# Decode attention and MLP on one core: weights loaded partition-major, K and P transposed on VectorE, scores by a block-diagonal q

## The chip, the cores and the metric

The kernel runs on one core of a Trainium2 chip. The metric is device time in microseconds (us). "Median" below is over the executions of one kernel. An execution counts as slow when it is over 1.5% above the fastest of the same kernel; comparisons use fast executions alone. A profile shows one execution, and its span is about 1.8 us shorter than the measured time (102.4 us against 104.2 us for the kernel before).

Names: PE is TensorE, PEld its weight loads, DVE VectorE, ACT ScalarE, POOL GpSimd, SP SyncE. A "q" after a name (ACTq) means that engine's own instruction stream, where it issues DMAs. L409 is line 409 of that kernel's own source, so the same work has other line numbers in other kernels.

## The reference

One token passes through attention over the last 4096 keys and through an MLP, both fed by the same normalised x, and both are added to x.

```python
# x (1,1,1024); wq (1024,4096); wo (4096,1024); w1 (1024,3584); w2 (3584,1024)
# caches (1,4,65536,128), only the last W=4096 rows are read; 32 q heads, 4 kv heads
xn = layernorm(x)
q  = (xn @ wq), as 32 heads of 128
o  = softmax(q . k^T * 128**-0.5) . v          # each kv head serves 8 q heads
y  = layernorm(xn)
out = x + o @ wo + (gelu(y @ w1 + b1) @ w2 + b2)
```

All data is bfloat16. The kernel must read 39.86 MB (the profile's own count): wq 8.4, w1 7.3, K 4.2, V 4.2, w2 7.3 and wo 8.4 MB. Each weight is used for one row only, so this is a streaming job with a chain of dependent steps hanging on it.

## The kernel before

The parts that matter. Weights are loaded row-block by row-block, so for wq, w1 and wo a run of contiguous memory for one partition is one row (8, 7 and 2 KB).

```python
WO_CHUNKS = [4, 4, 4, 4, 4, 4, 4, 3, 1]
W2_CHUNKS = [9, 9, 8, 2]
# SP issues the loads in this order: Wq, W1, K, V, W2, WO
for k in range(KC):
    sp.dma_start(WA[:, k * NQ:(k + 1) * NQ], A_wq[k * 128:(k + 1) * 128, :])
for k in range(KC):
    sp.dma_start(W1[:, k * F:(k + 1) * F], B_w1[k * 128:(k + 1) * 128, :])
# ... K and V: 32 keys of one partition are 8 KB in one run ...
# ... W2: nch rows of one partition in one run; WO:
sp.dma_start(WA[:, h0 * D:(h0 + nh) * D].rearrange("p (h n) -> p h n", h=nh),
             A_wo[h0 * 128:(h0 + nh) * 128, :].rearrange("(h d) n -> d h n", h=nh))
```

Rows become columns, and K becomes K transposed, on TensorE; the copies out of PSUM are shared by VectorE and ScalarE:

```python
for h in range(32):                                   # q row -> QT, 128x32
    pe.matmul(PSb[...], lhsT=Qrow[0:1, h*128:(h+1)*128], rhs=identb[0:1, 0:1], is_transpose=True)
for bb in range(16):                                  # 8 units of 16 K blocks
    pe.matmul(PSb[:, col0:col0+128], lhsT=KT[:, ...128 columns...], rhs=identb, is_transpose=True)
# ... copies PSUM -> KT on DVE and ACT ...
for g in range(HKV):                                  # scores: 128 small matmuls
    for b in range(NBLK):
        pe.matmul(PS[:, ...8 columns...], lhsT=KT[:, block b], rhs=QT[:, g*8:(g+1)*8])
# ... max, subtract, exp ...
w2_chunk_mms(pe, 0)          # 18 W2 matmuls sit here, under the softmax and before PV
for g in range(HKV):                                  # PV: 128 small matmuls
    for b in range(NBLK):
        pe.matmul(PS[:, ...8 columns...], lhsT=V[:, block], rhs=Pb[:, ...8 columns...])
# OT (128 x 32, one column per head) = PV result * 1/sum   -> already in the layout WO needs
for j in range(1, len(W2_CHUNKS)):
    w2_chunk_mms(pe, j)
# ... 64 WO matmuls with lhsT=OT[:, h:h+1], then copy and one output DMA
```

## Time and profile before

| | before |
|---|---|
| median time | 104.28 us (104.22 to 104.4) |
| span of the profile | 102.4 us |
| HBM read | 39.86 MB, 389 GB/s over the span |
| bulk packets in the trace: first start, last end | 1.75 us, 98.5 us |
| TensorE busy | 81.3 us, 79% |
| exp ends | 65.8 us |
| last matmul ends | 100.1 us |

The page of the kernel before, its 40 slices of 2.56 us each: busy tenths of TensorE, the granted TensorE clock in tenths, the mean busy share of the 16 DMA engines, and the rate.

```profile
PE   0021899999559998849999856489999999999991
...
PEclk9999999999999999995999955559995999999999
DMA  2999999999999999999999999999999999999910
GB/s 38 406 414 426 426 438 416 426 426 431 420 434 421 423 417 433 432 435 413 422 422 419 416 457 396 461 461 408 416 373 408 403 408 410 407 410 410 366 54 1
```

The DMA row is the one to read: 9 in every slice but the first and the last two. The stream never pauses. TensorE has free time, but next to none after the softmax, from 67 us on.

The page of the kernel before, the chain of waits that ended last, by engine and by line:

```profile
DMA 49%; PE 34%; SPq 14%; issue 1%; DVE 1%
DMA W<-in_B_w_dram 49%; PE PS L409 15%; PE PS L633 14%; SPq L160 10%; SPq L157 4%; PE PS L578 3%; PE PS L310 2%; DVE ROW L650 1%; PE PS L588 0%; PE PS L562 0%
```

Half of it is DMA, then the W2 matmuls (L409) and the WO matmuls (L633): the job is over when the last weights have come and been used.

The timeline of the kernel before; columns are start (us), length (us), engine, line, operation, output and inputs, shape and count, then idle time before it and what ended it.

```profile
56.90 3.41 PE L480 MATMUL PS<-QT,KV 128*128 128x8 bf16 x128 [0.42 <-DVE KV L454]
...
64.82 1.02 ACT L533 ACTIVATE Pb<-PS 128x1024 bf16<-128x1024 f32 x1 [7.26 <-DVE PS L524]
...
66.96 5.34 PE L409 MATMUL PS<-W,GT 128*1 128x512 bf16 x18 [1.88 <-DMA W<-in_B_w_dram]
...
72.30 3.37 PE L578 MATMUL PS<-Pb,KV 128*128 128x8 bf16 x128
...
75.93 10.05 PE L409 MATMUL PS<-W,GT 128*1 128x512 bf16 x38
...
85.81 14.31 PE L633 MATMUL PS<-WA,OT 128*1 128x512 bf16 x64
...
100.16 0.68 DVE L650 CAST ROW<-PS 1x512 bf16<-1x512 f32 x1 [23.64 <-PE PS L633]
```

Scores (L480) end at 60.3, exp (L533) at 65.8, 18 of the W2 matmuls run before PV (L578), PV takes 3.4 us, and from 66.96 to 100.1 TensorE is practically never idle. So the kernel before is balanced: the stream ends at 98.5 us, and TensorE has just caught up with it. Note that the 18 W2 matmuls took 5.34 us, which is 297 ns each, where 64 WO matmuls took 14.31 us, 224 ns each: their first part ran at the slower clock (the PEclk row has 5 up to the slice that ends at 69.1 us; the matmuls start 427 ns apart there, and 216 later).

### The profile page before, as it was taken

Reading aid. Unit: us, or ns where it says so; the run is one execution under the profiler, and the core shown is the slowest. Engines: PE = TensorE matmul, PEld = TensorE weight load, DVE = VectorE, ACT = ScalarE, POOL = GpSimd, SP = SyncE. Lnnn points to the kernel's source line nnn. Section 1 sums busy time; section 2 is a strip of 40 time slices with the busy share of each in tenths; the row PEclk is TensorE's granted clock in tenths of the full one; section 3 lists DMA queues with packets and bytes.
Section 4 is the critical chain, followed back from the end, with each engine's and each line's share of the span. In section 5 each row is a group of like instructions: output and inputs, shape, how many; then the busy total and the mean of one; then the engine's idle time right before and its main releaser. Section 6 shows DMA issues by size and latency. Waiting matters only on the chain.

```text
span 102.4 us, 1568 instructions
## 1 busy us (share of the span) xinstructions
PE 81.3 (79%) x700; PEld 41.1 (40%) x700; DVE 22.0 (21%) x47; ACT 14.1 (14%) x16; POOL 3.5 (3%) x14
## 2 busy tenths in 40 slices
PE   0021899999559998849999856489999999999991
PEld 0020333333123331339999753023872333333320
DVE  0016400000440000074759444540110000000002
ACT  5000510000420000053337400300000000000002
POOL 5700000000000000000000000000000000000000
PEclk9999999999999999995999955559995999999999
DMA  2999999999999999999999999999999999999910
GB/s 38 406 414 426 426 438 416 426 426 431 420 434 421 423 417 433 432 435 413 422 422 419 416 457 396 461 461 408 416 373 408 403 408 410 407 410 410 366 54 1
DMA packets 8407, 39.95 MB, mean 390 GB/s; under 512 B 721, under 2 KB 721, under 8 KB 5970
## 3 DMA queue, kind: packets, MB, share of 16 engines
q1 hardware_dynamic: 8274, 39.85, 94.5%
q8 instruction: 5, 0.08, 0.3%
q0 software_dynamic: 128, 0.01, 0.1%
HBM read 39.86 MB, written 0.00 MB: 389 GB/s over the span
## 4 chain that ended last, share of the span: by engine, by line
DMA 49%; PE 34%; SPq 14%; issue 1%; DVE 1%
DMA W<-in_B_w_dram 49%; PE PS L409 15%; PE PS L633 14%; SPq L160 10%; SPq L157 4%; PE PS L578 3%; PE PS L310 2%; DVE ROW L650 1%; PE PS L588 0%; PE PS L562 0%
## 5 line engine op out<-in xcount | busy, mean ns | idle before, releaser
L409 PE MATMUL PS<-W,GT 128*1 128x512 bf16 x56 | 15.4, 443 | 1.9 <-DMA W<-in_B_w_dram 1.9
L283 PE MATMUL PS<-WA,XNTb 128*1 128x512 bf16 x64 | 16.0, 417 | 0.3 <-DVE msy L244 0.3
L310 PE MATMUL PS<-W,YTb 128*1 128x512 bf16 x56 | 12.7, 379 | 3.5 <-DVE ROW L293 2.4
L633 PE MATMUL PS<-WA,OT 128*1 128x512 bf16 x64 | 14.3, 379 | 0.0
L439 PE MATMUL PS<-identb,KV 128*128 128x128 bf16 x128 | 9.1, 243 | 1.5 <-ACT ROW L336 1.5
L409 PEld LDWEIGHTS PS<-W,GT 128*1 128x1 bf16 x56 | 5.2, 95 | 12.1 <-issue 7.3
L283 PEld LDWEIGHTS PS<-WA,XNTb 128*1 128x1 bf16 x64 | 5.7, 90 | 10.2 <-issue 2.9
L439 PEld LDWEIGHTS PS<-identb,KV 128*128 128x128 bf16 x128 | 8.8, 111 | 1.6 <-ACT ROW L336 1.6
L310 PEld LDWEIGHTS PS<-W,YTb 128*1 128x1 bf16 x56 | 4.4, 83 | 11.9 <-DVE ROW L293 2.9
L633 PEld LDWEIGHTS PS<-WA,OT 128*1 128x1 bf16 x64 | 5.2, 84 | 8.9 <-DMA WA<-in_A_wo_dram 1.0
L454 DVE COPY KV<-PS 128x1024 bf16<-128x1024 bf16 x10 | 6.3, 685 | 2.3 <-PE PS L439 2.3
L466 ACT ACTIVATE KV<-PS 128x1024 bf16<-128x1024 bf16 x6 | 5.9, 1019 | 3.3 <-PE PS L439 3.3
L650 DVE CAST ROW<-PS 1x512 bf16<-1x512 f32 x1 | 0.7, 678 | 23.6 <-PE PS L633 23.6
L293 DVE CAST ROW<-PS 1x2048 bf16<-1x2048 f32 x1 | 2.3, 2278 | 14.8 <-PE PS L283 14.8
L177 PE MATMUL PS<-identb,X 8*128 8x8 bf16 x1 | 0.2, 181 | 6.5 <-DMA X<-in_A_x_dram 6.5
L644 ACT ACTIVATE ROW<-PS 1x512 bf16<-1x512 f32 x1 | 0.6, 586 | 34.3 <-PE PS L633 34.3
L298 ACT ACTIVATE ROW<-PS 1x2048 bf16<-1x2048 f32 x1 | 1.9, 1866 | 13.8 <-PE PS L283 13.8
L480 PE MATMUL PS<-QT,KV 128*128 128x8 bf16 x128 | 3.4, 167 | 0.4 <-DVE KV L454 0.4
L480 PEld LDWEIGHTS PS<-QT,KV 128*128 128x128 bf16 x128 | 3.3, 98 | 0.6 <-DVE KV L454 0.6
L336 ACT ACTIVATE ROW<-PS 1x1536 bf16<-1x1536 f32 x1 | 1.4, 1439 | 15.3 <-PE PS L323 15.3
L331 DVE COPY QT<-PS 128x32 bf16<-128x32 bf16 x1 | 0.2, 192 | 14.8 <-PE PS L323 14.8
L578 PE MATMUL PS<-Pb,KV 128*128 128x8 bf16 x128 | 3.4, 166 | 0.0
(77 smaller groups left out, 37.8 us busy)
## 6 DMA issues: line engine op xcount, KB each, us to landing
WA<-in_A_wq_dram SPq DMA_DIRECT2D x8, 1024.0 KB, 11.7
W<-in_B_w_dram SPq DMA_DIRECT2D x8, 896.0 KB, 25.4
WA<-in_A_wo_dram SPq DMA_DIRECT2D x7, 1024.0 KB, 15.1
W<-in_B_w_dram SPq DMA_DIRECT2D x2, 2304.0 KB, 26.2
KV<-in_A_k_cache_dram SPq DMA_DIRECT2D x4, 1024.0 KB, 26.2
KV<-in_A_v_cache_dram SPq DMA_DIRECT2D x4, 1024.0 KB, 27.1
W<-in_B_w_dram SPq DMA_DIRECT2D x1, 2048.0 KB, 33.1
WA<-in_A_wo_dram SPq DMA_DIRECT2D x1, 768.0 KB, 12.7
```

The source lines that it names most:

```text
L157: sp.dma_start(WA[:, k * NQ:(k + 1) * NQ], A_wq[k * 128:(k + 1) * 128, :]).then_inc(s_wq[k], 16)
L160: sp.dma_start(W1[:, k * F:(k + 1) * F], B_w1[k * 128:(k + 1) * 128, :]).then_inc(s_w1[k], 16)
L283: last = pe.matmul(PS[0:1, n * 512:(n + 1) * 512], lhsT=XNTb[:, k:k + 1], rhs=WA[:, k * NQ + n * 512: k * NQ + (n + 1) * 512], start=(k == ...
L293: STATE["d_qrow0"] = DVE.mark(dve.tensor_copy(Qrow[:, 0:2048], PS[0:1, 0:2048]))
L310: last = pe.matmul(PS[0:1, (n + 1) * 512:(n + 2) * 512], lhsT=YTb[:, k:k + 1], rhs=W1[:, k * F + n * 512: k * F + (n + 1) * 512], start=(k ...
L409: pe.matmul(PS[0:1, 6 * 512 + n * 512: 6 * 512 + (n + 1) * 512], lhsT=GT[:, c:c + 1], rhs=reg[:, n * 512:(n + 1) * 512], start=False, stop ...
L439: last = pe.matmul(PSb[:, col0: col0 + 128], lhsT=KT[:, g * W + b * 128: g * W + (b + 1) * 128], rhs=identb[:, :], is_transpose=True)
L454: last = dve.tensor_copy(KT[:, g * W + (hu * 16 + 8 * s_) * 128: g * W + (hu * 16 + 8 * s_ + 8) * 128], PSb[:, bk * 1024:(bk + 1) * 1024])
L466: STATE["a_ktcopy"][u] = ACT.mark(act.activation(out=KT[:, g * W + (hu * 16 + 8) * 128: g * W + (hu * 16 + 16) * 128], in_=PSb[:, bk * 102 ...
L480: last = pe.matmul(PS[:, bank_base + b * 8: bank_base + (b + 1) * 8], lhsT=KT[:, g * W + b * 128: g * W + (b + 1) * 128], rhs=QT[:, g * 8: ...
L578: last = pe.matmul(PS[:, 4 * 512 + g * REP: 4 * 512 + (g + 1) * REP], lhsT=V[:, (g * NBLK + b) * DH:(g * NBLK + b + 1) * DH], rhs=Pb[:, (g ...
L633: last = pe.matmul(PS[0:1, 6 * 512 + n * 512: 6 * 512 + (n + 1) * 512], lhsT=OT[:, h:h + 1], rhs=WA[:, h * D + n * 512: h * D + (n + 1) * ...
```

## The change

The intent is to make the DMA stream cheaper and to take the transposes off TensorE:

1. Each partition gets a block of consecutive rows of a weight (partition p holds rows 8p to 8p+7 of wq), so one run of wq is 16 KB where it was 8, of w1 14 where it was 7, and of wo 16 (10, 4 and 2 in the last chunks) where it was 2. W2, K and V were in long runs already. W1 now comes before Wq.
2. That order of rows wants x, h and the attention output in "p-major" order. Small DMAs from the ScalarE queue, on the chip or from HBM, spread rows over partitions: x, b1, h (HTb), q (Q2), and four for the attention output (OT).
3. K and P are transposed on VectorE in 32x32 blocks. The blocks are not put in their final place; instead a block-diagonal q (QBD) makes a 128-row matmul that gives the scores of all heads at once, and PV uses 32 matmuls of 512 columns with a mask that picks each head's own kv group.
4. The first W2 chunk no longer runs before PV: all W2 matmuls come after it.

The diff, cut to its core (`# ...` marks cuts; the setup, norms and GELU change little):

```diff
-WO_CHUNKS = [4, 4, 4, 4, 4, 4, 4, 3, 1]
-W2_CHUNKS = [9, 9, 8, 2]
+W1_CHUNKS = [2, 2, 2, 2]
+WQ_CHUNKS = [2, 2, 2, 2]
+W2_CHUNKS = [8, 8, 8, 4]
+WO_CHUNKS = [8, 8, 8, 5, 2, 1]
 # ... loads: W1 first, long runs
-            for k in range(KC):
-                sp.dma_start(WA[:, k * NQ:(k + 1) * NQ],
-                             A_wq[k * 128:(k + 1) * 128, :]).then_inc(s_wq[k], 16)
+    wq_p = A_wq.rearrange("(p k) n -> p (k n)", k=KC)
+    wo_p = A_wo.rearrange("(p j) n -> p (j n)", j=OC)
+            for i, c0, n in cuts(W1_CHUNKS):
+                sp.dma_start(W1[:, c0 * F:(c0 + n) * F], w1_p[:, c0 * F:(c0 + n) * F]).then_inc(s_w1[i], 16)
+            for i, c0, n in cuts(WQ_CHUNKS):
+                sp.dma_start(WQ[:, c0 * NQ:(c0 + n) * NQ], wq_p[:, c0 * NQ:(c0 + n) * NQ]).then_inc(s_wq[i], 16)
 # ... rows spread by DMAs of the ScalarE queue
+                act.dma_start(XB[:, :], x_p8).then_inc(s_x, 16)
+                act.dma_start(HTb[:, :], Hrow).then_inc(s_ht, 16)
+            act.dma_start(Q2[:, :], Qrow).then_inc(s_q2, 16)
 # ... K transposed on VectorE
-                    last = pe.matmul(
-                        PSb[:, col0: col0 + 128],
-                        lhsT=KT[:, g * W + b * 128: g * W + (b + 1) * 128],
-                        rhs=identb[:, :], is_transpose=True)
+            ST["d_kt0"] = DVE.mark(dve.transpose(KT(0), K(0)))
+            dve.wait_ge(s_q2, 16)
+            DVE.mark(dve.transpose(QT2[:, :], Q2[:, :]))
+            # ... 16 small copies QT2 -> QBD
+            for g in range(1, 4):
+                ST[f"d_kt{g}"] = DVE.mark(dve.transpose(KT(g), K(g)))
 # ... scores
-                    last = pe.matmul(
-                        PS[:, bank_base + b * 8: bank_base + (b + 1) * 8],
-                        lhsT=KT[:, g * W + b * 128: g * W + (b + 1) * 128],
-                        rhs=QT[:, g * 8:(g + 1) * 8],
+                        last = pe.matmul(
+                            bank(hf),
+                            lhsT=QBD[:, (g * 4 + b) * 128:(g * 4 + b + 1) * 128],
+                            rhs=KT(g).rearrange("p (t b i) -> p b t i", b=4, i=32)[:, b, hf * 16:(hf + 1) * 16, :],
 # ... P and PV; the first W2 chunk leaves its place before PV
+            ST["d_pt"] = DVE.mark(dve.transpose(PT, Pb))
-            w2_chunk_mms(pe, 0)
-                    last = pe.matmul(
-                        PS[:, 4 * 512 + g * REP: 4 * 512 + (g + 1) * REP],
-                        lhsT=V[:, (g * NBLK + b) * DH:(g * NBLK + b + 1) * DH],
-                        rhs=Pb[:, (g * NBLK + b) * REP:(g * NBLK + b + 1) * REP],
+            for t in range(T):
+                last = pe.matmul(
+                    PS[0:32, 2 * 512: 3 * 512],
+                    lhsT=PT[:, t * 32:(t + 1) * 32],
+                    rhs=V.rearrange("p (g t d) -> p t g d", g=HKV, t=T)[:, t, :, :],
+                # ... mask, 1/sum, reduce over groups -> O2 (32 heads x 128)
+                for q in range(4):
+                    act.dma_start(OT[q:128:4, :], O2[:, 32 * q:32 * (q + 1)]).then_inc(s_ot[q], 16)
```

## The prediction

> **What bounds it now.** The DMA stream. The slices show the 16 DMA engines 9/10 busy from about 2.4 us to 97 us of a 102.4 us span, at 373 to 461 GB/s (39.9 MB). The chain of waits ends DMA, W2 and WO matmuls, output. In the timeline the last eight WO matmuls start at 98.24, when the last chunk lands; the rest is matmuls, a copy, the output DMA. Measured time is 1.9 us above the span. TensorE has slack, but not much: after exp (ends 65.8) it runs 18+38 W2, 128 small PV and 64 WO matmuls almost without a gap to 100.1, waiting at WO's end about 1 us in all.
>
> **What the change removes.** Packets. The trace's packets take 84 ns at 2 KB, 309 at 8 KB, 611 at 16 KB, 686 at 18 KB: about 8.7 ns plus 0.0368 ns/B. Before has 60 runs per partition, after 26; with 8 partitions an engine that is 34 x 8 x 8.7 ns = 2.4 us less stream. I expect the last weights to land near 96 instead of 98.2. TensorE loses 128 K transposes (9 us), 60 row-to-column transposes (2.9 us), and the 128+128 small score and PV matmuls (3.4+3.4 us).
>
> **What it adds.** Four VectorE transposes of 128x4096 bf16 and one of 128x1024. The trace has none; [...] reduces of 128 and 1024 elements per partition (279 and 1225 ns)[...]; estimate 4.4 us each, 1.2 us for P. [...] 32 score and 32 PV matmuls of 512 columns at 0.216 us spacing (7 us each, more at half clock). W1 now comes before Wq.
>
> **Timeline of after (estimates).** Wq lands 40.7, its last 16 matmuls end 44.2, the q row copy (2.28 in the trace) ends 46.5. VectorE is then serial: K0 transpose, q spread, K1 to K3, to about 67. Last 8 score matmuls 69. Max, two small matmuls, bias, exp (1.2, then about 3.1) 73.7; P transpose 75. PV, starting at half clock as W2 did at 67 in before, about 9 us: 84. Then W2 56 x 0.216 = 12.1 and WO 64 x 0.216 = 13.8, all behind PV in program order: 110. Copy and output: span 112.4, time 114.
>
> So nothing of the 2.4 us DMA gain is on the final path. The bottleneck moves to q -> VectorE transposes -> softmax -> PV, then 26 us of already landed W2 and WO. Softmax ends 8 us later than before, and W2's first chunk no longer fills the softmax wait, which alone costs several us.
>
> **Prediction.** 114 us, range 109 to 118. Faster by over 2%: 0.06; within 2%: 0.11; slower: 0.83.
>
> **What would show it.** DMA ends near 96 and then idles over 10 us while PE works. K transposes about 4.4 us each back to back, 47 to 67. TensorE half idle in 45 to 75 with clock near 0.5; solid from 75 to 110. The chain lists VectorE K transposes and PE W2, WO, hardly DMA. WO matmuls wait for no DMA, nor for the attention column DMAs (four, done near 89).
>
> **What would make it wrong.** [...] If q's spread DMA queues behind bulk packets (611 ns each) for more than 5 us, it adds delay directly. If strided 64 KB pitch reads ran slower, DMA would end later, but 14 us of slack would hide that.

The sum is: q row 46.5, K3 67, scores 69, exp 73.7, P 75, PV 84, last matmul 110, span 112.4, time 114 us. Of its terms, the step from 46.5 to 67 holds four transposes of 4.4 us and 2.9 us for the q spread and its copies; the q DMA was counted as hidden. The 4.4 and 1.2 us are estimates: a line through the two reduces of before that are named (279 ns for 128 elements per partition, 1225 ns for 1024) gives 4.5 us for 4096 and 1.2 for 1024. That a transpose goes at the pace of a reduce was not shown before the run. Two conditions came to this: transposes in half the time, a tie near 104 us; slower ones, 118 or more.

## The result

| | before | after |
|---|---|---|
| median time, same rounds | 104.22 us (104.21 to 104.4) | 115.83 us (115.16 to 117.66) |
| ratio of fast runs (95% interval) | 1 | 1.1071 (1.1036 to 1.1105) |
| span of the profile | 102.4 us | 115.9 us |
| last bulk packet ends | 98.5 us | 98.1 us |
| P ready for PV | 65.8 us | 78.3 us |
| last matmul ends | 100.1 us | 113.7 us |

The changed kernel is slower by 10.7%. A ratio here is the mean time of one kernel's fast runs over that of the other's fast runs of the same rounds, so it is not quite the ratio of the medians quoted. Two ratios taken on different chips are compared through the kernel before, which ran beside each.

One caution: the profiled execution of the changed kernel is one of its two slow ones (117.66 us). Where a duration matters, the experiment "a_wo_short" serves as a fast counterpart: its program differs only in how WO is fetched, its time is the same, and its profile is of a fast run (span 114.0 us). It is called the fast counterpart below.

The page of the kernel after, its slices (2.9 us each), the same four rows:

```profile
PE   0011399997499999200665549309999999999992
...
PEclk9999999999959999955589855965699999999999
DMA  4999999999999999999999999999999993000000
GB/s 84 386 421 427 437 420 452 430 418 430 441 413 420 399 427 421 418 421 424 424 444 424 430 438 418 404 444 435 418 430 435 402 395 144 0 0 0 0 0 1
```

The DMA row is 9 until about 95 us and then 0 for six slices, while PE still shows 9. From slice 17 to 27 (46 to 78 us) PE reads 2 0 0 6 6 5 5 4 9 3 0, where before it read 9 9 9 9 8 5 6 4 8 9 9 9 9 in that time, and PEclk is often 5: the matrix engine waits, and is slow when it gets something.

The page of the kernel after, the chain of waits:

```profile
PE 61%; DVE 23%; DMA 11%; issue 2%; ACT 1%; DVEq 0%; ACTq 0%
PE PS L342 14%; PE PS L282 12%; PE PS L532 12%; DVE BREG L401 12%; PE PS L522 10%; PE PS L481 8%; DMA XB<-in_A_x_dram 6%; DMA Q<-CREG 5%; PE PS L419 3%; DVE CREG L356 2%; DVE BREG L296 2%; DVE QBD L394 1%; DVE BREG L469 1%; PE PS L208 1%; DVE MX L431 1%
```

DMA fell from 49% to 11% of the chain, and that 11% is the landing of x and of q, two tiny transfers. VectorE went from 1% to 23%. So the bottleneck is no longer the stream.

The timeline of the kernel after (columns as before): K0's transpose and the DMA that spreads q, the three other K transposes, the last scores, exp, the transpose of P, PV, W2, the spread of the attention output, WO.

```profile
48.47 4.42 DVE L386 STREAM_TRANSPOSE BREG<-BREG 128x4096 bf16<-128x4096 bf16 x1
...
48.63 0.58 ACTq L362 DMA_DIRECT2D Q<-CREG  x1
53.98 0.30 DVE L388 STREAM_TRANSPOSE QT<-Q 32x128 bf16<-32x128 bf16 x1 [1.09 <-DMA Q<-CREG]
...
56.04 13.55 DVE L401 STREAM_TRANSPOSE BREG<-BREG 128x4096 bf16<-128x4096 bf16 x3
...
69.64 3.41 PE L419 MATMUL PS<-BREG,QBD 128*128 128x512 bf16 x8 [1.71 <-DVE BREG L401]
...
75.86 1.11 ACT L464 ACTIVATE BREG<-PS,NM 128x1024 bf16<-128x1024 f32 x1 [27.74 <-DVE NM L459]
77.01 1.25 DVE L469 STREAM_TRANSPOSE BREG<-BREG 128x1024 bf16<-128x1024 bf16 x1 [1.18 <-ACT BREG L464]
...
78.31 9.37 PE L481 MATMUL PS<-BREG 128*32 128x512 bf16 x32 [2.68 <-DVE BREG L469]
...
87.57 12.25 PE L522 MATMUL PS<-CREG,GT 128*1 128x512 bf16 x56
...
89.97 3.02 ACTq L513 DMA_DIRECT2D OT<-O  x4
...
99.66 13.98 PE L532 MATMUL PS<-AREG,OT 128*1 128x512 bf16 x64
```

Read from bottom to top: WO (L532) starts when W2 (L522) ends, with no wait; W2 starts when PV (L481) ends; PV waits for P's transpose; the scores wait for the last K transpose; the K chain starts when the q row is copied, at 48.5. It is one serial chain of 65 us, of which the last 26 us are W2 and WO, whose weights have all landed before their turn comes.

The same steps in the timeline of the fast counterpart (a_wo_short): the three K transposes, PV, W2 and WO.

```profile
55.17 13.55 DVE L402 STREAM_TRANSPOSE BREG<-BREG 128x4096 bf16<-128x4096 bf16 x3
...
75.94 9.79 PE L482 MATMUL PS<-BREG 128*32 128x512 bf16 x32 [2.68 <-DVE BREG L470]
...
85.63 12.25 PE L523 MATMUL PS<-CREG,GT 128*1 128x512 bf16 x56
...
97.72 13.98 PE L533 MATMUL PS<-AREG,OT 128*1 128x512 bf16 x64
```

The 11.6 us between before and this fast run split in two. P is ready for PV at 75.94 where exp ended at 65.84: 10.1 us. From there to the last matmul it is 35.8 us (to 111.7) where it was 34.3 us (to 100.1): 1.5 us. PV takes 9.8 us in place of 3.4, but W2 and WO now run without a wait and at full clock (219 and 218 ns each), which gives most of that back.

The small transfers deserve a look. The page's list of DMA issues of the kernel before: output and input, issuing engine, count, KB each, median us from issue to landing.

```profile
X<-in_A_x_dram POOLq DMA_DIRECT2D x1, 2.0 KB, 5.2
```

The same list of the kernel after:

```profile
OT<-O ACTq DMA_DIRECT2D x4, 2.0 KB, 6.2
XB<-in_A_x_dram ACTq DMA_DIRECT2D x1, 2.0 KB, 7.1
...
HTb<-BREG ACTq DMA_DIRECT2D x1, 7.0 KB, 10.5
Q<-CREG ACTq DMA_DIRECT2D x1, 8.0 KB, 5.3
```

A 2 KB transfer takes 6 to 7 us and the 7 KB of h 10.5 us, beside a bulk stream that keeps the DMA engines busy (mean share 1.02 from 40 to 60 us of after). The trace's packets show two parts. First, nothing moves for 3.8 to 3.9 us after the issue (h: issued at 30.60, first packet at 34.41; q: 48.63 and 52.51; attention output: 89.97 and 93.84), where the output DMA, alone at the end, starts 0.75 us after its issue. What holds the first packet back beside the stream is not shown. Then the packets themselves go out slowly: h's 128 packets of 56 bytes (11 ns each, 27 at most) went out between 34.4 and 38.8 (two stragglers until 40.0). If the 16 engines shared them evenly, that is eight each and one about every 0.6 us, close to the time of one 16 KB bulk packet (611 to 613 ns), the size that ran beside them. Which engine sent which packet is not in the trace. The spread took longer where the bulk packets beside it were longer: the 128 packets of the attention output went out within 2.6 us beside bulk packets of 2 KB (a_wo_short), within 3.3 us beside 2 to 10 KB, the short tail of WO (after), and within 7.0 us where most were of 16 KB (a_no_kt, a_wq_first). So, by these runs, the long runs of this change have a price: the small transfers beside them are slower.

### The profile page after: what moved, and what is told of

Read it like the earlier page. It is cut to its first block, busy times and chain, and to the rows that moved or that the text cites. A ratio compares the mean times of both kernels' runs of the same rounds, so it can differ in the third digit from the quotient of the medians.

```text
span 115.9 us, 799 instructions
## 1 busy us (share of the span) xinstructions
PE 79.5 (69%) x315; PEld 29.5 (25%) x315; DVE 36.4 (31%) x58; ACT 8.4 (7%) x10; POOL 3.0 (3%) x13
## 4 chain that ended last, share of the span: by engine, by line
PE 61%; DVE 23%; DMA 11%; issue 2%; ACT 1%; DVEq 0%; ACTq 0%
PE PS L342 14%; PE PS L282 12%; PE PS L532 12%; DVE BREG L401 12%; PE PS L522 10%; PE PS L481 8%; DMA XB<-in_A_x_dram 6%; DMA Q<-CREG 5%; PE PS L419 3%; DVE CREG L356 2%; DVE BREG L296 2%; DVE QBD L394 1%; DVE BREG L469 1%; PE PS L208 1%; DVE MX L431 1%
## 5 line engine op out<-in xcount | busy, mean ns | idle before, releaser
L419 PE MATMUL PS<-BREG,QBD 128*128 128x512 bf16 x32 | 11.5, 529 | 12.1 <-DVE QBD L394 6.6
L342 PE MATMUL PS<-AREG,XNTb 128*1 128x512 bf16 x64 | 15.7, 410 | 2.4 <-DVE BREG L296 2.4
L282 PE MATMUL PS<-CREG,YTb 128*1 128x512 bf16 x56 | 14.3, 423 | 1.8 <-DVE YTb L270 1.8
L532 PE MATMUL PS<-AREG,OT 128*1 128x512 bf16 x64 | 14.0, 379 | 0.0
L401 DVE STREAM_TRANSPOSE BREG<-BREG 128x4096 bf16<-128x4096 bf16 x3 | 13.3, 4445 | 0.3
L522 PE MATMUL PS<-CREG,GT 128*1 128x512 bf16 x56 | 12.2, 379 | 0.0
L481 PE MATMUL PS<-BREG 128*32 128x512 bf16 x32 | 9.4, 465 | 2.7 <-DVE BREG L469 2.7
L342 PEld LDWEIGHTS PS<-AREG,XNTb 128*1 128x1 bf16 x64 | 5.6, 89 | 12.4 <-DVE BREG L296 2.9
L282 PEld LDWEIGHTS PS<-CREG,YTb 128*1 128x1 bf16 x56 | 5.0, 91 | 10.7 <-issue 3.0
L532 PEld LDWEIGHTS PS<-AREG,OT 128*1 128x1 bf16 x64 | 5.4, 84 | 8.4
L522 PEld LDWEIGHTS PS<-CREG,GT 128*1 128x1 bf16 x56 | 4.6, 84 | 7.1
L481 PEld LDWEIGHTS PS<-BREG 128*32 128x32 bf16 x32 | 3.6, 114 | 8.1 <-issue 3.0
L386 DVE STREAM_TRANSPOSE BREG<-BREG 128x4096 bf16<-128x4096 bf16 x1 | 4.4, 4423 | 0.0
L309 DVE TENSOR_TENSOR HT<-HTb,B1T 128x28 f32<-128x28 bf16 x1 | 0.2, 186 | 10.7 <-DMA HTb<-BREG 10.7
```

What stands on the lines that cost most here:

```text
L282: last = pe.matmul(row(n), lhsT=YTb[:, k:k + 1], rhs=W1[:, k * F + n * 512: k * F + (n + 1) * 512], start=(k == 0), stop=(k == KC - 1))
L342: last = pe.matmul(row(n), lhsT=XNTb[:, k:k + 1], rhs=WQ[:, k * NQ + n * 512: k * NQ + (n + 1) * 512], start=(k == 0), stop=(k == KC - 1))
L386: ST["d_kt0"] = DVE.mark(dve.transpose(KT(0), K(0)))
L401: ST[f"d_kt{g}"] = DVE.mark(dve.transpose(KT(g), K(g)))
L419: last = pe.matmul(bank(hf), lhsT=QBD[:, (g * 4 + b) * 128:(g * 4 + b + 1) * 128], rhs=KT(g).rearrange("p (t b i) -> p b t i", b=4, i=32)[ ...
L481: last = pe.matmul(PS[0:32, 2 * 512: 3 * 512], lhsT=PT[:, t * 32:(t + 1) * 32], rhs=V.rearrange("p (g t d) -> p t g d", g=HKV, t=T)[:, t, ...
```

## The experiments

Twelve kernels ran. Those with a_ start from the changed kernel, those with b_ from the kernel before. Theory A: the time is the serial chain q, VectorE transposes, softmax, PV, W2, WO; the stream has slack. Rivals: B, the new way of fetching is what is slow; C, the small spread DMAs set a second limit, near enough to hide gains in the chain. The chip's check passed all of them, even a_wo_short and a_no_kt, which are wrong, so it says nothing of attention. The author also emulated the arithmetic of the others in numbers, on inputs on which attention matters, and found them right.

| run | what | median us | ratio to before (95%) |
|---|---|---|---|
| after | | 115.83 | 1.1071 (1.1036 to 1.1105) |
| a_wo_short | WO in 2 KB runs | 115.89 | 1.1085 (1.1058 to 1.1111) |
| a_no_kt | no K transposes | 113.07 | 1.0721 (1.0665 to 1.0776) |
| a_w2_gap | first W2 chunk before PV | 116.65 | 1.1177 (1.1161 to 1.1194) |
| a_pv_small | PV as 128 small matmuls | 116.44 | 1.1145 (1.1115 to 1.1174) |
| a_gap_sel | a_w2_gap, spread by matmul | 111.08 | 1.0616 (1.0585 to 1.0646) |
| a_pv_sel | a_pv_small, spread by matmul | 113.41 | 1.0777 (1.0739 to 1.0814) |
| a_wq_first | Wq before W1 | 111.67 | 1.0692 (1.0650 to 1.0734) |
| a_best | the four mends together | 104.63 | 1.0047 (0.9992 to 1.0102) |
| a_best_fine | a_best, WO in smaller chunks | 103.86 | 0.9936 (0.9917 to 0.9955) |
| a_best_warm | a_best_fine, two W2 columns earlier | 103.91 | 0.9958 (0.9939 to 0.9976) |
| b_w2_early | before, W2's first chunk cut in two and started earlier | 104.23 | 0.9999 (0.9969 to 1.0030) |
| b_both | b_w2_early, long WO runs, spread by matmul | 105.04 | 1.0075 (1.0043 to 1.0106) |

The medians are over all executions, slow ones too; the ratios are of fast ones. So a_no_kt and a_pv_sel, with three slow executions in six, look slower by their medians than by their ratios.

### a_wo_short: is the way of fetching what is slow?

WO is fetched in the old 2 KB runs. The rows then land in another order, so the output is wrong; nothing else changes.

```diff
-                sp.dma_start(WO[:, c0 * D:(c0 + n) * D], wo_p[:, c0 * D:(c0 + n) * D]).then_inc(s_wo[i], 16)
+                sp.dma_start(WO[:, c0 * D:(c0 + n) * D].rearrange("p (h n) -> p h n", h=n),
+                             A_wo[c0 * 128:(c0 + n) * 128, :].rearrange("(h d) n -> d h n", h=n)).then_inc(s_wo[i], 16)
```

> The changed kernel with the long WO runs undone: WO read in 2 KB runs as before (rows permuted, so the output is wrong on purpose). My theory: the DMA stream is off the critical path, so the WO stage drops from about 430 to 408 GB/s, the last weights land about 1 us later (near 99 instead of 98), and the time stays within 0.5 us of the changed kernel's 115.2 to 115.8 us. Rival (the weight stream still sets the end): 1 to 2 us slower than the changed kernel.

Measured: 115.89 us, ratio 1.1085, the same as after. The last bulk packet ended at 100.1 us in place of 98.1. The windows of 80 to 90 us, first of before, then after, then a_wo_short. Columns: the window and its length, busy us (and number of instructions) of PE, PEld, DVE, ACT and POOL, then the granted clock, the busy share of the DMA engines, and GB/s.

```profile
80.00:90.00 10.00, 10.00 (x48) 3.94 (x47) 0.00 (x0) 0.00 (x0) 0.00 (x0) 1.00 1.05 408
```

```profile
80.00:90.00 10.00, 10.00 (x43) 4.13 (x42) 2.22 (x5) 0.00 (x0) 0.00 (x0) 0.85 1.00 426
```

```profile
80.00:90.00 10.00, 10.00 (x46) 4.10 (x45) 2.08 (x4) 0.00 (x0) 0.00 (x0) 0.93 1.05 387
```

In this program the long runs are worth 2 us at the end of the stream (426 GB/s against 387), and nothing of it shows in the time (1.1071 against 1.1085, with intervals that overlap). Rival B falls as far as WO's run length goes: the end of the stream is not what is slow, and making it faster buys nothing. The order of the loads is another matter (a_wq_first, below).

### a_no_kt: are the VectorE transposes the cost?

The four K transposes are taken out and the scores read K untransposed (wrong).

```diff
-            ST["d_kt0"] = DVE.mark(dve.transpose(KT(0), K(0)))
 # ... and those of g = 1 to 3
-                pe.wait_ge(DVE.sem, ST[f"d_kt{g}"])
+                pe.wait_ge(s_k[g], 16)
-                            rhs=KT(g).rearrange(...)
+                            rhs=K(g).rearrange(...)
```

> The changed kernel without the four K transposes; the score matmuls read K as it landed (wrong output on purpose, same sizes and same number of matmuls). My theory: the transposes K1 to K3 are on the path, 13.4 us between the q spread (56.0) and the last score group (69.6); without them the 32 score matmuls run back to back from about 56, end near 64.6 instead of 73.1, and everything behind moves: 8 to 9 us faster, about 107 us. Rival (q's late arrival and TensorE's own work set the path, the transposes are hidden beside matmuls): under 3 us faster.

Measured: 113.07 us, ratio 1.0721, that is 3.2% or about 3.6 us faster than after, well short of the 8 to 9 us expected. The timeline of a_no_kt: scores, W2, the issue of the four spread DMAs, WO.

```profile
55.21 9.79 PE L414 MATMUL PS<-BREG,QBD 128*128 128x512 bf16 x32 [6.85 <-DVE QBD L393]
...
79.25 12.25 PE L517 MATMUL PS<-CREG,GT 128*1 128x512 bf16 x56
...
81.64 3.32 ACTq L508 DMA_DIRECT2D OT<-O  x4
...
93.81 15.66 PE L527 MATMUL PS<-AREG,OT 128*1 128x512 bf16 x64 [2.31 <-DMA OT<-O]
```

The scores end at 65.0, 8.1 us earlier than in the profile of after and 5.7 us earlier than in the fast counterpart, although all 32 now run in one row behind q (part of them at the slow clock). W2 starts at 79.25 and ends at 91.5. Then comes something new: WO waits 2.31 us, for the DMA that spreads the attention output. It was issued at 81.64 and its 64-byte packets were still going out at 92.46. WO then starts at the slow clock: 15.66 us in place of 13.98. Against the fast counterpart W2 starts 6.4 us earlier (79.25, 85.63) but WO ends only 2.2 us earlier (109.5, 111.7): the wait and the slow clock took 4.0 us (2.31 and 1.68; this profile is a slow run besides). It is the first sign of theory C. Of the 10.1 us by which P comes later than in before, 5.7 go with the K transposes (P is ready at 70.25 here, at 75.94 in the fast counterpart) and 4.4 stay.

### a_w2_gap: W2's first chunk under the softmax

The 16 matmuls of the first W2 chunk go back before PV, where before had them.

```diff
+            pe.wait_ge(DVE.sem, ST["d_GT"])
+            w2_mms(pe, 0)
             pe.wait_ge(DVE.sem, ST["d_pt"])
 # ... PV ...
-            for i, c0, nc_ in cuts(W2_CHUNKS):
+            for i in range(1, len(W2_CHUNKS)):
```

> The changed kernel with W2's first 16 matmuls moved ahead of PV in program order, into the wait for exp and the P transpose (correct output). My theory: the work that stands behind softmax is too much for TensorE, so filling a 2.7 us idle gap and keeping the clock up through PV gains 2 to 4 us: 111.5 to 113.5 us. Rival (softmax chain alone sets the end): delaying PV by 1 to 4 us makes it 0 to 3 us slower.

Measured: 116.65 us, ratio 1.1177: slower by 1.0% than after, where 2 to 4 us of gain were expected. The timeline of a_w2_gap: the rest of W2, the issue of the spread, WO.

```profile
83.83 8.79 PE L169 MATMUL PS<-CREG,GT 128*1 128x512 bf16 x40
...
86.23 2.44 ACTq L524 DMA_DIRECT2D OT<-O  x4
...
96.08 15.27 PE L538 MATMUL PS<-AREG,OT 128*1 128x512 bf16 x64 [3.45 <-DMA OT<-O]
```

W2 now ends at 92.6, five us sooner than in the fast counterpart, but WO cannot start before 96.08, when the spread has landed; 3.45 us are waited away. The hope for the clock came true in PV, which took 7.1 us here and 9.8 in the fast counterpart, but after the wait the clock was at half until 98.7, so WO takes 15.27 us. The work moved into the gap was simply waited for later. In the kernel after the two limits lie close together: W2 ends at 99.66, and the last of the four spread DMAs landed at 97.7 (issued at 91.79, 5.9 us to landing by the trace); in the fast counterpart it is 97.72 and 95.2. This is why the changed kernel itself shows no wait there. One caution: this profile is of the fastest of six executions (115.39 us), which is no slower than after; the other five took 116.6 to 116.8, so the 1% itself is not in this trace.

### a_pv_small: PV in the old form

PV as 128 matmuls of 8 columns, with a transpose on TensorE to get heads onto partitions; the rest as in after.

```diff
-            for t in range(T):
-                last = pe.matmul(
-                    PS[0:32, 2 * 512: 3 * 512],
-                    lhsT=PT[:, t * 32:(t + 1) * 32],
-                    rhs=V.rearrange("p (g t d) -> p t g d", g=HKV, t=T)[:, t, :, :],
-                    start=(t == 0), stop=(t == T - 1))
+            for g in range(HKV):
+                for t in range(T):
+                    last = pe.matmul(
+                        PS[:, 2 * 512 + g * REP: 2 * 512 + (g + 1) * REP],
+                        lhsT=V[:, (g * T + t) * DH:(g * T + t + 1) * DH],
+                        rhs=PT[:, t * 32 + g * REP: t * 32 + (g + 1) * REP],
+                        start=(t == 0), stop=(t == T - 1))
 # ... copy PS -> OD, 16 W2 matmuls, transpose OD on TensorE, times 1/sum -> O2
```

> The changed kernel with PV as in the kernel before: V as the loaded weight, 128 matmuls of 8 columns, instead of 32 of 512 columns; the result is transposed back to rows for the same on-chip spread (correct output). PV took 9.4 us here and 3.4 us before. My theory: PV lies on the path, so 4 to 6 us faster, 109.5 to 111.5 us (W2 may then start at half clock and give 1.5 to 2 us back). Rival (PV is hidden behind the wait for the attention spread or for weights): no change.

Measured: 116.44 us, ratio 1.1145, slower than after by 0.7%. PV itself fell from 9.4 to 3.58 us. But the 16 W2 matmuls after it took 5.24 us in place of 3.61 (they took 3.61 in a_w2_gap at full clock; here the clock record shows half from 69.8 to 83.5, through the small matmuls and beyond), and WO again waited 2.37 us for the spread, until 96.71, and then took 15.66 us. Same pattern as the two runs before. The timeline of a_pv_small, WO:

```profile
96.71 15.66 PE L543 MATMUL PS<-AREG,OT 128*1 128x512 bf16 x64 [2.37 <-DMA OT<-O]
```

### a_gap_sel and a_pv_sel: take the spread away

Here the wait is tested by removing its cause. The spread of O2 (32 heads x 128) to OT is done by four matmuls with one-hot matrices in place of four DMAs; one run on top of a_w2_gap, one on top of a_pv_small.

```diff
+            for q in range(4):     # SEL[h, q*128 + 4h + q] = 1
+                last = pe.matmul(bank(4, 32), lhsT=SEL[:, q * 128:(q + 1) * 128],
+                                 rhs=O2[:, q * 32:(q + 1) * 32], start=(q == 0), stop=(q == 3))
+            ST["d_ot"] = DVE.mark(dve.tensor_copy(OT[:, :], bank(4, 32)))
-                    act.dma_start(OT[q:128:4, :], O2[:, 32 * q:32 * (q + 1)]).then_inc(s_ot[q], 16)
```

> The w2_gap kernel, with the four attention-spread DMAs replaced by four one-hot matmuls of 32 columns and a copy (correct output). New theory after the first four runs: the four spread DMAs, [...] land only when the WO stream ends (about 94 to 98 us whatever the issue time), so that no work saved ahead of them can start WO before that: a second floor right behind the first. Without them W2 ends near 92.5 and WO follows at once at full clock: end near 106.5, time 110 to 111.5 us. Rival (the misses of the first runs came from the clock falling to half at unlucky times): still 114 us or more, WO starting no earlier than 95.

> The pv_small kernel with the same one-hot spread instead of the four DMAs (correct output). New theory: pv_small's W2 matmuls ended at 94.3 and WO waited 2.4 us for the spread and then ran partly at half clock (15.7 instead of 14.0 us); without the wait 112 to 113 us, that is 3 to 4 us faster than pv_small's 116.4. Rival (clock only): within 1 us of pv_small.

Measured: a_gap_sel 111.08 us, ratio 1.0616, which is 5.0% below a_w2_gap (1.0616 over 1.1177). a_pv_sel 113.41 us, ratio 1.0777, which is 3.3% below a_pv_small (1.0777 over 1.1145). These pairs ran on different chips, so they are compared by their ratios to before. Both profiles fell on slow runs. The timeline of a_gap_sel: the four matmuls, and WO.

```profile
89.43 0.26 PE L534 MATMUL PS<-O,SEL 32*128 32x32 bf16 x4
...
94.80 13.98 PE L554 MATMUL PS<-AREG,OT 128*1 128x512 bf16 x64
```

Four matmuls of 0.26 us in all do what took the DMAs 5.6 to 8.3 us each in the other runs, and WO (13.98 us) has no wait before it. This shows theory C for these programs: with the DMA spread in place, moving W2 into the gap is worth nothing or less; without it, the same move and the mend together are worth 4.1% against after (1.0616 over 1.1071). The one-hot spread alone, put into after, was not run; WO does not wait for the spread there, so no gain would be expected.

### a_wq_first: q earlier

The loads of Wq and W1, and their matmuls, change places, as before had them; the row copy of h goes to ScalarE and the GELU on VectorE behind the K transposes, so that K's chain is not held up.

```diff
-            for i, c0, n in cuts(W1_CHUNKS):
-                sp.dma_start(W1[:, c0 * F:(c0 + n) * F], w1_p[:, c0 * F:(c0 + n) * F]).then_inc(s_w1[i], 16)
             for i, c0, n in cuts(WQ_CHUNKS):
                 sp.dma_start(WQ[:, c0 * NQ:(c0 + n) * NQ], wq_p[:, c0 * NQ:(c0 + n) * NQ]).then_inc(s_wq[i], 16)
+            for i, c0, n in cuts(W1_CHUNKS):
+                sp.dma_start(W1[:, c0 * F:(c0 + n) * F], w1_p[:, c0 * F:(c0 + n) * F]).then_inc(s_w1[i], 16)
 # ... the matmuls, row copies and spreads of q and h change places likewise
-            ST["a_hrow"] = ACT.mark(act.activation(out=Hrow[:, 0:1536], in_=row(0, 3), func=ACTF.Copy))
+            ST["a_hrow"] = ACT.mark(act.activation(out=Hrow[:, :], in_=row(0, 7), func=ACTF.Copy))
 # ... q spread, QBD, then on VectorE:
+            for g in range(4):
+                dve.wait_ge(s_k[g], 16)
+                ST[f"d_kt{g}"] = DVE.mark(dve.transpose(KT(g), K(g)))
 # ... and only then the GELU of h
```

> The changed kernel with Wq loaded and used before W1, as in the kernel before (correct output; the spread DMAs stay). Theory: q is then ready by about 36 us, K0's transpose starts when K0 lands (about 43) and not after the q copy (48), so K3's ends near 62 instead of 69 and the softmax chain is about 6 us earlier; but the attention spread DMAs still land only near 94 to 96, so the time falls by only 2 to 3 us, to 112 to 114 us. If the spread were no floor: about 109 us. If q's place were not on the path: no change.

Measured: 111.67 us, ratio 1.0692, 3.4% below after (1.0692 over 1.1071). The timeline of a_wq_first: the four K transposes, the issue of the spread, WO.

```profile
44.02 18.10 DVE L342 STREAM_TRANSPOSE BREG<-BREG 128x4096 bf16<-128x4096 bf16 x4 [1.61 <-DMA BREG<-in_A_k_cache_dram]
...
81.04 3.37 ACTq L499 DMA_DIRECT2D OT<-O  x4
...
93.23 13.97 PE L518 MATMUL PS<-AREG,OT 128*1 128x512 bf16 x64 [2.33 <-DMA OT<-O]
```

The K transposes now wait for K alone: they start at 44.0 and run back to back. P is ready at 69.3 (75.9 in the fast counterpart, 78.3 in the slow profile), W2 ends at 90.9. Once more WO waits, 2.33 us, for a spread that was issued at 81.04 and was awaited until 93.23. (Here the clock stayed full behind the wait: WO took 13.97 us.)

### a_best and a_best_fine: the mends together

a_best joins Wq first, the W2 chunk before PV, small PV and the one-hot spread. (Their edits are those shown above.) a_best_fine differs from it in one line:

```diff
-WO_CHUNKS = [8, 8, 8, 5, 2, 1]
+WO_CHUNKS = [4, 4, 4, 4, 4, 4, 4, 2, 1, 1]
```

> All repairs together: Wq first, W2's first 16 matmuls in the softmax gap, PV as 128 small matmuls, one-hot spread in place of the spread DMAs; long runs and VectorE transposes stay (correct output). Theory: TensorE then has W2 done by about 85 to 87 and WO is bound by the weights again, which land near 98: end of matmuls 98.5 to 100, time 102 to 104.5 us, within 2 percent of the kernel before, perhaps 1 percent faster. If the VectorE transposes by themselves were what makes the changed kernel slow, it stays above 108 us.

> a_best with WO cut into chunks of 4, 4, 4, 4, 4, 4, 4, 2, 1, 1 rows instead of 8, 8, 8, 5, 2, 1. In a_best TensorE waited 1.3 us for the third chunk (landed 93.4) and then had 32 matmuls, 7.1 us, left after it. Theory: with finer chunks the WO matmuls follow the weights and end about 0.5 us after the last chunk lands near 98: 102.5 to 103.3 us, 1 to 2 percent faster than the kernel before. If TensorE's own work was the limit: no change, 104.5.

Measured: a_best 104.63 us, ratio 1.0047, no different from before; WO waited 1.29 us at 93.38 for its third chunk of 8 rows and then had 32 matmuls (7.07 us) left. So the limit is the stream again, and the size of the last chunks decides how much TensorE work is left when they land. The timeline of a_best, the second half of WO:

```profile
93.38 7.07 PE L547 MATMUL PS<-AREG,OT 128*1 128x512 bf16 x32 [1.29 <-DMA AREG<-in_A_wo_dram]
```

Two of its six executions (105.90 and 105.91) lie just under the 1.5% that makes an execution slow; by the other four the ratio is 1.000. With smaller chunks, a_best_fine takes 103.86 us, ratio 0.9936 (0.9917 to 0.9955): it beats both kernels, by 0.6% and by 10%. The 0.6% is small, and of fast executions alone: two of its six were slow (105.83 and 106.17), and none of the eleven of before beside it. The timeline of a_best_fine, K transposes and WO:

```profile
43.85 18.09 DVE L360 STREAM_TRANSPOSE BREG<-BREG 128x4096 bf16<-128x4096 bf16 x4 [2.69 <-DMA BREG<-in_A_k_cache_dram]
...
85.66 13.98 PE L547 MATMUL PS<-AREG,OT 128*1 128x512 bf16 x64
```

The last bulk packet ends at 98.0, and WO at 99.6. VectorE's 18 us of K transposes are all still there; they now fit under the stream. The four mends gave 3.4% (Wq first), 4.1% (gap and spread) and, for small PV with the spread, 2.7% (1.0777 over 1.1071) against after, which cannot just be added, as the spread is in two of them; together they gave 9.3% (1.0047 over 1.1071).

### a_best_warm: is the slow clock after the scores worth anything?

Four W2 matmuls go right behind the scores, in the hope of keeping the clock up through the softmax.

```diff
-W2_CHUNKS = [8, 8, 8, 4]
+W2_CHUNKS = [2, 6, 8, 8, 4]
             ST["pe_sc"] = PE.mark(last)
+            pe.wait_ge(DVE.sem, ST["d_GT"])
+            w2_mms(pe, 0)
```

> a_best_fine with W2 in chunks of 2, 6, 8, 8, 4 rows, the first (4 matmuls) placed right after the scores, where TensorE waits 1.3 us for the maximum (correct output). In a_best_fine TensorE ran from 67.8 to 99.7 without a wait, 1.8 us of it lost to half clock, while the last weights landed near 98.0. Theory: TensorE's work behind the scores is now the limit, so moving 0.9 us of it into the wait, perhaps with an earlier full clock, gives 0.5 to 1.5 us: 102.4 to 103.4 us. If the weight stream is the limit, no change from 103.9; if the four matmuls only delay the maximum, 0.5 us slower.

Measured: 103.91 us, ratio 0.9958 (0.9939 to 0.9976), no change from a_best_fine. WO waits 0.52, 0.59 and 0.64 us for its chunks, the last of them at 96.29, so time saved on TensorE is spent waiting for weights.

### b_w2_early and b_both: do parts of the change help the old kernel?

b_w2_early cuts W2's first chunk in the kernel before in two, so that the same 18 matmuls can start sooner under the softmax (at 64.2 us in place of 67.0), moves the matmuls of the x and b2 rows right behind the scores, and makes the chunks at the end smaller. b_both also fetches WO in long runs, with a transpose and the one-hot matmuls to bring OT into that order.

```diff
 # b_w2_early against before
-WO_CHUNKS = [4, 4, 4, 4, 4, 4, 4, 3, 1]
-W2_CHUNKS = [9, 9, 8, 2]
+WO_CHUNKS = [4, 4, 4, 4, 4, 4, 4, 2, 1, 1]
+W2_CHUNKS = [4, 5, 9, 8, 2]
 # ... the four matmuls of the x and b2 rows move to right after the scores
             w2_chunk_mms(pe, 0)
+            w2_chunk_mms(pe, 1)
 # b_both against b_w2_early
-                    WA[:, h0 * D:(h0 + nh) * D].rearrange("p (h n) -> p h n", h=nh),
-                    A_wo[h0 * 128:(h0 + nh) * 128, :].rearrange("(h d) n -> d h n", h=nh),
+                    WA[:, h0 * D:(h0 + nh) * D],
+                    wo_p[:, h0 * D:(h0 + nh) * D],
 # ... among the W2 chunks, transpose OT and spread it:
+            STATE["pe_oT"] = PE.mark(pe.matmul(
+                PSb[0:32, 2 * 1024: 2 * 1024 + 128], lhsT=OT[:, :], rhs=identb[:, :], is_transpose=True))
+            STATE["d_o2"] = DVE.mark(dve.tensor_copy(O2[:, :], PSb[0:32, 2 * 1024: 2 * 1024 + 128]))
 # ... the one-hot matmuls of a_gap_sel -> OTP, which the WO matmuls read
```

> The kernel before, loads unchanged (WO in 2 KB runs), with less standing behind softmax: the four x and b2 matmuls moved right after the scores, W2 in chunks of 4, 5, 9, 8, 2 with the first two ahead of PV, and WO's tail cut 2, 1, 1 instead of 3, 1. Theory: TensorE gets ahead of the weights, the end becomes the last landing (98.2 to 98.5) plus 0.5 us: 102.8 to 103.5 us, about 1 percent faster than before.

> b_w2_early with WO in long runs per partition as in the changed kernel, and the attention column spread by a transpose and four one-hot matmuls (correct output). Theory: only here, where the weight stream sets the end, do the long runs count: the WO stage goes from 408 to about 430 GB/s, last landing 0.5 to 1.1 us earlier than in b_w2_early, so 0.5 to 1.1 us faster than it: 101.8 to 102.7 us, about 2 percent faster than before. If long runs are worth the 2.4 us of the prediction: 100.5 to 101 us. If nothing: the same as b_w2_early.

Measured: b_w2_early 104.23 us, ratio 0.9999; the percent that was expected did not come. TensorE ran at half clock from 60.4 to 67.2 and from 74.1 to 80.9 and WO (86.16 to 100.2) ran without a wait, so TensorE had no slack to give. b_both 105.04 us, ratio 1.0075: 0.8% slower than b_w2_early, where 2% faster than before was expected. Its last bulk packet ended at 98.80, that of b_w2_early at 98.76: in this pair the long runs moved the stream's end by nothing, though the rate from 80 to 90 us was 423 against 408 GB/s. WO waited 0.62 us at 96.75 with 16 matmuls left. Both expectations missed. About half of the 0.8 us lies outside the profiled span: b_both's measured times are 2.15 to 2.27 us above its spans, those of b_w2_early 1.75 to 1.88, and of all other kernels 1.68 to 1.97. Why, and what the rest is, is not explained.

## Why the prediction was right

The call (slower, 114 us) and the mechanism held; the measured median of 115.83 us lies in the range (fast executions 115.16 to 115.83).

Step by step, times in us; "fast" is the profile of a_wo_short, "profiled" the slow run of after:

| step | predicted | fast | profiled |
|---|---|---|---|
| Wq matmuls end | 44.2 | 45.6 | 46.3 |
| q row copied | 46.5 | 47.8 | 48.5 |
| K3 transposed | 67 | 68.7 | 69.6 |
| scores end | 69 | 70.7 | 73.1 |
| P transposed | 75 | 75.9 | 78.3 |
| PV (duration) | 9 | 9.8 | 9.4 |
| W2, WO (durations) | 12.1, 13.8 | 12.2, 14.0 | 12.2, 14.0 |
| last matmul ends | 110 | 111.7 | 113.7 |

- **"Estimate 4.4 us each, 1.2 us for P."** Right, and the largest term. K's transposes took 4423 to 4445 ns each, P's 1245 ns; the slope is (4423 - 1245)/(4096 - 1024) = 1.03 ns per element per partition. The two reduces in the trace of before, from which the 4.4 and 1.2 us can be worked out, have the slope (1225 - 279)/(1024 - 128) = 1.06 ns. So the transposes have nearly the slope of the reduces; before the run that was an assumption.
- **"All behind PV in program order: 110."** Right: W2 and WO follow PV without a wait, and DMA is idle for six slices at the end.
- **"Nothing of the 2.4 us DMA gain is on the final path."** Right that nothing reaches the time (a_wo_short). The size was wrong. The term was "34 x 8 x 8.7 ns = 2.4 us less stream" (the 8 is 128 partitions over 16 engines, taken as even); the stream ended only 0.4 us earlier (98.5 to 98.1). The 8.7 ns came from the duration of single packets, but packets overlap: with 2 KB runs the window of 80 to 90 us shows a DMA share of 1.05, more than one engine's worth of packet time. By rates, the 8.39 MB of WO at 426 in place of 408 GB/s save 0.9 us (20.6 less 19.7), not the 1.8 that the formula gives for WO's 26 runs fewer per partition (26 x 8 x 8.7 ns); and the start was slower (357 against 379 GB/s from 2 to 8 us, where the small loads go out beside the bulk). What the long runs are worth stays open: 2.0 us in a_wo_short against after, nothing in b_both against b_w2_early.
- **The small miss, 1.7 us at the last matmul (110 against 111.7).** Wq's matmuls ended 1.4 us later than predicted, the transposes from the q copy to K3 took 0.4 us more, the way from there to P 0.8 us less, PV and what follows 0.8 us more. In the first term the prediction took Wq's landing for 40.7; in a_pv_small the last 16 Wq matmuls waited for it until 41.6. The late x (7.1 us to landing, first W1 matmul at 13.85) costs at most 1.0 us in the profile of after and 0.3 in the fast one, since 41.6 plus 3.6 us for 16 matmuls is 45.2 in any case.
- **"K0 transpose, q spread, K1 to K3."** The q DMA was counted as hidden behind the first transpose. It took 5.3 us from issue to landing, so 1.1 us stuck out behind K0 (the 1.09 in L388's line). A mis-sized term: the prediction's last paragraph had named it as a risk, for more than 5 us, and it came out just beyond that. That it queued behind bulk packets, the reason given there, is not shown: 3.9 us passed before the first packet, and then all 32 packets started within 0.6 us.
- **"Nor for the attention column DMAs (four, done near 89)."** Wrong step, hidden in the result. They were issued from 89.97 on, their packets went out until 97.2, and the last of them landed at 97.7, not near 89. That WO does not wait for them in after was right with 1.9 us to spare (2.5 in the fast counterpart), by luck and not by the reason given, and every run that shortened the chain ahead of WO and kept them ran into this wait (2.3 to 3.5 us).
- **"W2's first chunk no longer fills the softmax wait, which alone costs several us."** Wrong as put. Putting that chunk back alone gained nothing (1% slower), as WO then waited 3.45 us for the spread. It counts once the spread is gone. The word "alone" was the mistake: it added up costs on one path and did not ask what the second latest path was.

So the kernel lost its time as predicted, and the experiments add the second floor under it.

## What stays open

The value of long runs (0 to 2 us, above); why b_both is 0.8% slower than b_w2_early; what delays the first packet of a small transfer beside the stream by 3.8 us; and how much each mend gives alone in the final version, as they lean on each other. What small matmuls do to the clock is read from timelines, not from a run made for it alone, and the timelines differ: behind the small PV the 16 W2 matmuls took 5.24 us in a_pv_small, where the clock was at half when PV began, and 3.61 us in a_best, a_best_fine and a_best_warm, where W2 matmuls ran just before PV. (The clock records of before and after last multiples of 3.413 us. PV filled one such stretch, 76.7 to 80.1, in a_pv_small and none in these three.)

## What to carry to other kernels

Before you make a stream cheaper, see whether something else will end last once the new work is in: here a gain of at most 2 us at the stream's end was paid for with 10 us on the chain to the softmax. When you move work off one path, look for the path that comes second; a wait that reads 0.0 today may be 2 us from a wait that counts. Beside a stream that kept the DMA share at 1.0 and above, a small DMA took 5.2 us and more here: in after 5.3 to 6.3 us in 32 packets (q, and each of the four of the attention output) and 7.1 to 11.0 in 128 (x, h, b1), though in a_wq_first q took 7.2 and h 6.8. The 128 packets of the attention output, four times 32, went out within 2.6 us beside bulk packets of 2 KB and within 7.0 beside mostly 16 KB. Four one-hot matmuls of 0.26 us in all could replace those four DMAs.

## What else the traces show

- Packets of small transfers. On the ScalarE queue of after the trace lists one packet for each small run (128 of 16 bytes for x, 128 of 64 bytes for the attention output), while b1 from the GpSimd queue in before came in 16 packets of 448 bytes, eight runs of 56 bytes each. In after b1 took 128 packets of 56 bytes from the ScalarE queue, and 11.0 us to landing in place of 5.7.
- Time to landing. The four small loads of before, from the GpSimd queue, took 5.2 to 5.7 us from issue to landing beside the stream. On the ScalarE queue it was 5.2 us (q in a_wo_short) and more, 3.8 to 3.9 of them before the first packet in the transfers of after that started from SBUF.
- Rates. In the window of 80 to 90 us 2 KB runs gave 387 (a_wo_short) and 408 GB/s (before), and 16 KB runs 426 (after). The first and last are of the same program but for the runs; why the two of 2 KB differ is not shown.
- The clock. In before and after its records last multiples of 3.413 us, and matmuls of 512 columns come 427 or 216 ns apart. In a_pv_small the stretch from 76.7 to 80.1 us was filled by 128 matmuls of 8 columns (PV, 76.53 to 80.11), and the clock stayed at half in the next one, so 16 W2 matmuls took 5.24 us (327 ns each); in after the stretch from 79.6 to 83.0 was filled by matmuls of 512 columns (PV, 78.31 to 87.6), and the clock was full from 83.0 on (W2: 12.25 us for 56, 219 ns each). What decides it is not shown.
